# Stage four of a prime-factor Fourier transform in quarter-array matmuls, in a fused mixing and mixture-of-experts kernel

## The chip, the cores and the metric

The kernel runs on one core of one Trainium2 chip. The metric is the device time of one execution in microseconds (us). The kernel before takes 1470.89 us, the median of three runs (1468.29, 1470.89 and 1471.23).

The core has a matmul engine (PE, a 128 by 128 array whose results go to PSUM), three engines for elementwise work (DVE, ACT and POOL), and a queue engine (SP) that starts nearly all transfers (DMAs). PSUM has eight banks of 128 partitions by 512 float32. Everything here is float32. In the profile one matmul of the program shows as two PE instructions, each with a weight load of its own ("PEld").

## The reference

Two blocks follow each other: a filter in the frequency domain along the sequence, then a mixture of experts with one expert for each row.

```python
# x: (8, 2496, 256); filt_r, filt_i: (1249, 256)
X = np.fft.rfft(x, axis=1)
y = np.fft.irfft(X * (filt_r + 1j * filt_i)[None], n=2496, axis=1)

# rows: y as (19968, 256); 8 experts; w1: (8, 256, 1024), w2: (8, 1024, 256)
logits = rows @ w_gate
expert = argmax(logits, axis=1)
gate = softmax(logits)[expert]
out = gate * (relu(rows @ w1[expert]) @ w2[expert])
```

## The kernel before

**The transform.** 2496 is 39 times 64, and 39 and 64 have no common factor, so the transform of one batch is four stages of small matrix products. Stage a multiplies over the 39 (table `tas`), stage b over the 64 (`tbs`) and then with the filter on DVE, stage c goes back over the 64 (`tcs`), and stage d goes back over the 39 (`tds`). The 64 positions along the other axis are taken three at a time: 22 groups, 21 of three positions and one of a single position. A group of three has 3 x 39 = 117 rows of data (`TP`) and 3 x 40 = 120 rows of spectrum (`TK`: 20 cosine and 20 sine parts for each position). One chunk is four groups; a batch has five chunks of four groups and one of two, the last of which holds the single position.

Stage d (`stage_d`, lines 579 to 596) takes a chunk of the spectrum `ui`, 120 partitions by 4 x 256, and issues one matmul for each two groups: 120 rows deep, 128 columns of `tds`, 512 wide, into one PSUM bank. `evac` (line 409) copies the bank to `yo` on DVE or ACT, whichever is planned to be done first. The chunk of two groups issues two matmuls of 256, one 120 deep and one 40 deep, because its second group has only one position.

Between the stages the data goes through DRAM: `zd` after stage a, `ud` after stage c, both written by `move` and read back by `load_z` and `load_u` (lines 514 to 527), all on the queue of SP. Batch 0 stays on the chip instead (`first_a`, `turn_z`, `first_c`, `turn_u`).

**Routing.** For batches 3 to 7 (`by_blocks`), DVE transposes `yo` in 32 by 32 blocks (`turn_y`), `block_logits` multiplies with the gate weights in matmuls that use 32 columns each and lie beside each other on the array (tile `bank<-yt,wb`), and `block_back` turns the logits back. `route` (a generator, line 738 on) finds each row's expert and its place. Then POOL writes each group's rows to `rows` in DRAM, ordered by expert, with one indirect DMA per group (`scatter`), 22 per batch of up to 117 rows. A row of `rows` is 256 values, eight copies of its token's number and eight of its gate (`DR = D + 16`).

**The experts.** `rows_in` loads a tile of up to 512 rows of one expert (the numbers and gates go to `ng`, eight buffers), `weights` loads its weights. Most tiles' first product is seven block products in place of eight (`hidden_by_quarters`), each with an add on DVE out of PSUM (`hT<-bank,hT`), after sums of weights and rows on POOL. The second product is `result`, four row blocks of eight matmuls. Once all transform steps are issued (`late`), tiles of 512 rows take seven block products for it too (`result_by_quarters`), with sums of `w2` on POOL (`w2_sums`, tile `tsum`). Finished rows go to the output by an indirect DMA on POOL (`send`).

**Order of work.** Each engine runs its instructions in order, and the kernel's Python writes that order out. `slot(k)` lists the steps of slot k: stages b and c of batch k, stage a of batch k+1, stage d and routing of batch k-1. A planner (`Order`, lines 125 to 234) keeps an estimated time for each engine; the main loop picks the next step whose data and PSUM bank it expects to be ready, and fills PE between transform steps with expert products, as far as `share` allows. `bank()` hands out the PSUM bank that it expects to be free first. The DMA queue of SP is in order too: an entry that waits for a buffer holds back those behind it.

**The start.** `load_filters(c)` loads four of the 20 filter columns at a time. The real parts go to the first 64 partitions of `ht` and ACT copies them to the other 64 (`turn_z`, line 630). The imaginary parts come in pieces on 64 partitions each; POOL multiplies them with the signs `sgs`, two chunks ahead.

Of the kernel before, what the change touches and what calls it, by code (L numbers as in the profile page):

```python
# [34 lines left out]
TK = NB * NS  # L35
DH = D // P
# [4 lines left out]
NJ = D // CT  # L41

# [13 lines left out]
def dft_tables():  # L56
# [24 lines left out]

    ids = np.zeros((NB, N1, NG))
    valid = np.zeros((NB, N1, NG))
    for j in range(NB):
# [3 lines left out]

    by_block = np.zeros((4, CT, NG + 2))
    by_block.reshape(P, NG + 2)[:TP, :NG] = valid.reshape(TP, NG)  # L90
# [5 lines left out]
        "ta": ta.reshape(TP, TK),  # L96
        "tb": tb,
        "tc": tc,
        "td": np.pad(td.reshape(TK, TP), ((0, 0), (0, P - TP))),
        "sg": np.concatenate([sg[:, :NF // 2], sg[:, NF // 2:]]),  # L100
        "ids": ids.reshape(TP, NG),
        "valid": np.concatenate([np.pad(valid.reshape(TP, NG), ((0, P - TP), (0, 0))), by_block], axis=1),
    }


def lay_x(x):

    out = np.zeros((x.shape[0], P, NG, D), x.dtype)
    q = np.arange(N1)
    for j in range(NB):  # L110
        for i in range(len(range(j, N2, NB))):
            out[:, j * N1:(j + 1) * N1, i] = x[:, token(q, NB * i + j)]
    return out
# [11 lines left out]
class Order:  # L125
# [25 lines left out]
    @staticmethod  # L151
    def parts(a):

        if a.name[:3] != "ht_":
            return [a.name]
        row, at = divmod(a.offset, a.ap[0][0])
        return [f"{a.name}/{h}/{k}" for h in ((0, 1) if a.ap[0][1] == P else (row // (P // 2),))
                for k in range(at // (2 * D), at // (2 * D) + (a.ap[1][1] + 1) // 2)]
# [20 lines left out]
    def count(self, engine, op, args, named):  # L179
# [31 lines left out]
        else:  # L211
            if out is None:
                took = 0.8 if engine == "sync" else 0.02
            elif engine == "tensor":
# [3 lines left out]
                took = max(0.1, 0.00085 * n) if op == "transpose" else max(0.216, 0.00169 * n) if rows > 32 else 0.00045 * n  # L218
                took *= 2.0 if start < self.slow else 1.0
# [31 lines left out]
class Slots:  # L251
# [3 lines left out]
    def freed(self, name, tag):  # L255
# [3 lines left out]
        if tag in self.live and name in self.live[tag]():  # L259
            return 1e9  # L260
# [33 lines left out]
def kernel(  # L294
# [12 lines left out]
    ids: bass.AP,  # L307
    valid: bass.AP,
# [25 lines left out]
    TR = E * TE  # L334

    dram = open_pool(ctx, name="dram", bufs=1, space=DRAM)
    zd = [dram.tile([N2, NS, D], F32, tag=f"z{b % 2}", name="zd") for b in range(B)]
    ud = [dram.tile([N2, NS, D], F32, tag=f"u{b % 2}", name="ud") for b in range(B)]


    DR = D + 16
    rowsd = dram.tile([TR, DR], F32, tag="rows", name="rows")

# [15 lines left out]

    tas = cst.tile([TP, TK], F32, name="tas")  # L360
    tbs = cst.tile([P, P], F32, name="tbs")
    tcs = cst.tile([P, P], F32, name="tcs")
    tds = cst.tile([TK, P], F32, name="tds")
# [15 lines left out]
    ids0 = cst.tile([TP, NG], F32, name="ids0")  # L379
    vld = cst.tile([P, 2 * NG + 2], F32, name="vld")  # L380
# [12 lines left out]
    ps.live["bank"] = lambda: ()  # L393
# [25 lines left out]
    def load_filters(c):  # L419
        f0, n = FH[c]  # L420
        if c == 0:
            nc.sync.dma_start(out=tbs, in_=tb)
            nc.sync.dma_start(out=sgs, in_=sg)
        nc.sync.dma_start(out=ht[:HP, f0:f0 + n], in_=filt[:HP, f0:f0 + n, :])
        half, f1 = divmod(f0, NF // 2)
        rows = slice(half * HP, (half + 1) * HP)
        nh = min(n, NF // 2 - f1)
        parts = [(rows, slice(f1, f1 + nh), slice(NF + f1, NF + f1 + nh))]
        if nh < n:
            parts.append((slice(HP, P), slice(0, n - nh), slice(NF, NF + n - nh)))  # L430
        for r, fs, at in parts:
            nc.sync.dma_start(out=ht[r, at], in_=filt[r, at, :])
            signs.append((c, ht[r, at], sgs[r, fs, None].to_broadcast((HP, fs.stop - fs.start, D))))
        if c == 0:
            nc.sync.dma_start(out=tcs, in_=tcm)

    def load_rest():
        nc.sync.dma_start(out=tds, in_=td)
# [33 lines left out]
    def columns(ap, i0, n):  # L472

        rows = ap.rearrange("t s d -> (t s) d")
        m = min(n, NG - 1 - i0)
        yield TK, slice(0, m), rows[i0 * TK:(i0 + m) * TK, :].rearrange("(i p) d -> p i d", p=TK)
        if m < n:
            yield NS, slice(m, n), rows[(NG - 1) * TK:, :].rearrange("(i p) d -> p i d", p=NS)

# [22 lines left out]
    def by_part(ap):  # L502

        return ap.rearrange("t (c f) d -> (t c) f d", c=2)

# [8 lines left out]
    def load_z(b, c):  # L514
        f0, n = FH[c]
        zi = fin(("z", b, c))
        nc.sync.dma_start(out=zi[:, :n], in_=by_part(zd[b])[:, f0:f0 + n, :])

    def load_u(b, c):
        i0, n = CH[c]  # L520
        ui = fin(("u", b, c))
        for r, m, v in columns(ud[b], i0, n):
# [5 lines left out]

    def stage_a(b, c):
        i0, n = CH[c]  # L530
        xt = ins.pop(("x", b, c))
        zo = sb.tile([TK, 4, D], F32, tag="st", name="zo", bufs=4)
        for j in range(0, n, 2):
            p = bank()
            mm(p[:TK, :], lhsT=tas, rhs=xt[:TP, j:j + 2, :], start=True, stop=True)
            evac(zo[:, j:j + 2, :], p[:TK, :].rearrange("p (t d) -> p t d", t=2), 512)
        for r, m, v in columns(zd[b], i0, n):
# [4 lines left out]
    def stage_b(b, f):  # L542
# [6 lines left out]
        mm(p, lhsT=tbs, rhs=zi[:, j:j + 2, :], start=True, stop=True)  # L549
# [13 lines left out]

    def stage_c(b, f):
# [6 lines left out]
        mm(p, lhsT=tcs, rhs=ys, start=True, stop=True)  # L571
        evac(uo[:, j:j + 2, :], p.rearrange("p (i d) -> p i d", i=2), 512)
        if j == 2:
            f0 = f - 2
            move(by_part(ud[b])[:, f0:f0 + 4, :], uo)
# [3 lines left out]
    def stage_d(b, c):  # L579
# [7 lines left out]
        yo = outs["o", b, c] = sb.tile([P, 4, DR], F32, tag="y", name="yo", bufs=YB)  # L587
        for j in range(0, n, 2):
            p = bank()
            if i0 + j + 2 < NG:  # L590
                mm(p, lhsT=tds, rhs=ui[:TK, j:j + 2, :], start=True, stop=True)
# [6 lines left out]


# [12 lines left out]
    def first_a(c):  # L612
        i0, n = CH[c]
        xt = ins.pop(("x", 0, c))
        for j in range(0, n, 2):
            p = bank()[:, :4 * TK]
            for h in range(DH):
                for i in range(2):
                    mm(p[:, (2 * h + i) * TK:(2 * h + i + 1) * TK], lhsT=xt[:TP, j + i, h * P:(h + 1) * P], rhs=tas,
# [954 lines left out]
```

## Time and profile before

| what | value |
|---|---|
| median of three runs | 1470.89 us |
| the profiled execution | 1474.5 us |
| its span, first to last instruction | 1472.8 us |
| mean granted PE clock | 0.992 |
| PE instructions | 7828, and as many weight loads |
| stage d: matmul instructions 512 wide from `ud` (batches 1 to 7) | 140 |
| stage d: 256 wide, 120 deep and 40 deep | 14 and 14 |
| DVE and ACT copies of `yo` out of PSUM | 6 and 82 |
| scatters to `rows` | 176, and 8 of padding |

The profile is of one execution. Its page gives busy times of each engine, the share of 40 equal slices, the DMA queues, the chain of work that ended last, and groups of instructions with their mean durations. Matmuls overlap: a mean of 606 ns for a matmul instruction contains its way through the array, and the next one starts earlier. What one costs in a row of many is therefore read from the timeline, from one start to the next. Batch 3's first block transposes are at 301.7 us of the span, and stage d of batch 7 reads its last spectrum at 877.1 us, so stage d of batches 3 to 7 lies in the stretch from 300 to 900 us.

### The profile page before, as it was taken

Reading aid. Unit: us, or ns where it says so; the run is one execution under the profiler, and the core shown is the slowest. Engines: PE = TensorE matmul, PEld = TensorE weight load, DVE = VectorE, ACT = ScalarE, POOL = GpSimd, SP = SyncE. Lnnn points to the kernel's source line nnn. Section 1 sums busy time; section 2 is a strip of 40 time slices with the busy share of each in tenths; the row PEclk is TensorE's granted clock in tenths of the full one; section 3 lists DMA queues with packets and bytes.
Section 4 is the critical chain, followed back from the end, with each engine's and each line's share of the span. In section 5 each row is a group of like instructions: output and inputs, shape, how many; then the busy total and the mean of one; then the engine's idle time right before and its main releaser. Section 6 shows DMA issues by size and latency. Waiting matters only on the chain.

```text
span 1472.8 us, 25703 instructions
## 1 busy us (share of the span) xinstructions
PE 1438.4 (98%) x7828; PEld 1148.5 (78%) x7828; DVE 835.8 (57%) x1818; ACT 480.5 (33%) x1005; POOL 818.9 (56%) x1214
## 2 busy tenths in 40 slices
PE   8998999999999999999999999999999999999998
PEld 5553555777577777777787778889999999999997
DVE  4666568335766574566757554566878775531110
ACT  3553443233232333222223232222232322223332
POOL 3434355525456654565375567647989878831111
PEclk9999999999999999999999999999999999999999
DMA  9749798887786576557345644548665424456661
GB/s 255 243 156 339 250 323 257 271 260 222 246 246 189 169 253 180 150 167 251 105 126 151 205 117 132 149 128 244 175 186 154 133 77 139 135 191 176 173 192 42
DMA packets 216383, 278.19 MB, mean 189 GB/s; under 512 B 124131, under 2 KB 163708, under 8 KB 216245
## 3 DMA queue, kind: packets, MB, share of 16 engines
q1 hardware_dynamic: 197125, 233.19, 53.7%
q0 software_dynamic: 19120, 43.33, 8.5%
q8 instruction: 66, 1.08, 0.3%
q14 instruction: 72, 0.59, 0.1%
HBM read 196.45 MB, written 80.64 MB: 188 GB/s over the span
## 4 chain that ended last, share of the span: by engine, by line
PE 85%; DMA 6%; DVE 4%; issue 2%; POOL 1%; SPq 1%; ACT 1%; POOLq 0%; DVEq 0%; ACTq 0%
PE bank L246 85%; DMA fin<-in_x_dram 2%; DMA fin<-ud 2%; DVE yw L246 1%; DVE ys L246 1%; DMA ud<-uo 1%; DMA fin<-zd 1%; SPq L246 1%; POOL out_dram L246 0%; DVE hT L246 0%; DMA w1t<-in_moe_w_dram 0%; DMA ng<-rows 0%; ACT hT L246 0%; DMA zd<-zo 0%; DMA xg<-rows 0%
## 5 line engine op out<-in xcount | busy, mean ns | idle before, releaser
L246 DVE TENSOR_TENSOR hT<-bank,hT 128x512 f32<-128x512 f32 (+1 forms) x504 | 300.8, 626 | 165.4 <-PE bank L246 77.7
L246 PE MATMUL bank<-w2t,hT 128*128 128x256 f32 (+1 forms) x1984 | 387.5, 350 | 2.4 <-DVE hT L246 1.4
L246 PEld LDWEIGHTS bank<-w2t,hT 128*128 128x128 f32 x1984 | 335.1, 190 | 53.0 <-issue 11.7
L246 PE MATMUL bank<-xT,w1t 128*128 128x256 f32 (+1 forms) x1728 | 316.3, 329 | 0.2 <-DVE hT L246 0.2
L246 POOL DMA_INDIRECT out_dram<-ys,ng x161 | 161.5, 1003 | 271.6 <-ACT ys L246 136.7
L246 PEld LDWEIGHTS bank<-xT,w1t 128*128 128x128 f32 x1728 | 265.4, 192 | 32.4 <-issue 8.3
L246 ACT ACTIVATE hT<-hT 128x1024 f32<-128x1024 f32 (+1 forms) x144 | 135.0, 959 | 390.5 <-DVE hT L246 387.5
L246 POOL DMA_INDIRECT rows<-yo,row x176 | 181.9, 1034 | 74.8 <-POOL yo L246 38.5
L246 ACT ACTIVATE ys<-bank,ng 128x256 f32<-128x256 f32 x104 | 49.3, 474 | 303.9 <-PE bank L246 235.2
L246 PE MATMUL bank<-sums,wsum 128*128 128x256 f32 (+1 forms) x576 | 135.6, 358 | 0.0
L246 PE MATMUL bank<-w2s,hT 128*128 x592 | 132.6, 379 | 0.0
L246 PEld LDWEIGHTS bank<-w2s,hT 128*128 128x128 f32 x592 | 110.3, 190 | 13.8
L246 PEld LDWEIGHTS bank<-sums,wsum 128*128 128x128 f32 x576 | 100.5, 190 | 17.7 <-issue 6.8
L246 POOL TENSOR_TENSOR wsum<-w1t 128x256 f32<-128x256 f32 x72 | 56.5, 785 | 82.2 <-PE bank L246 57.7
L246 DVE STREAM_TRANSPOSE xT<-xg 128x512 f32<-128x512 f32 (+2 forms) x126 | 57.4, 493 | 54.6 <-PE bank L246 51.4
L246 DVE TENSOR_TENSOR ys<-bank,ht 128x512 f32<-128x512 f32 x80 | 54.8, 685 | 52.2 <-PE bank L246 42.9
L246 PE MATMUL bank<-fin,tas 117*120 117x512 f32 x154 | 77.3, 622 | 6.9 <-DMA fin<-in_x_dram 6.7
L246 PE MATMUL bank<-fin,tds 120*128 120x512 f32 (+1 forms) x168 | 76.1, 573 | 3.9 <-DMA fin<-ud 3.3
L246 PE MATMUL bank<-fin,tbs 128*128 128x512 f32 x140 | 72.6, 605 | 5.4 <-DMA fin<-zd 5.4
L246 PE MATMUL bank<-ys,tcs 128*128 128x512 f32 x140 | 73.3, 611 | 4.2 <-DVE yw L246 3.4
L246 ACT ACTIVATE hT<-bank 128x128 f32<-128x128 f32 (+1 forms) x191 | 57.6, 303 | 52.5 <-PE bank L246 42.9
L246 PE MATMUL bank<-xT,wsum 128*128 128x256 f32 (+1 forms) x288 | 67.8, 358 | 0.2 <-ACT yo L246 0.2
(171 smaller groups left out, 1766.6 us busy)
## 6 DMA issues: line engine op xcount, KB each, us to landing
w1t<-in_moe_w_dram SPq DMA_DIRECT2D x126, 512.0 KB
w2t<-in_moe_w_dram SPq DMA_DIRECT2D x68, 512.0 KB
fin<-in_x_dram SPq DMA_DIRECT2D x39, 512.0 KB
fin<-zd SPq DMA_DIRECT2D x35, 512.0 KB
ud<-uo SPq DMA_DIRECT2D x35, 512.0 KB
fin<-ud SPq DMA_DIRECT2D x35, 512.0 KB
zd<-zo SPq DMA_DIRECT2D x35, 480.0 KB
xg<-rows SPq DMA_DIRECT2D x112, 128.0 KB
```

What stands on the lines that cost most here:

```text
L246: return real(*args, **named)
```

## The change

- **Stage d of batches 3 to 7** uses the symmetry of cosine and sine. Real and imaginary parts are kept apart: 60 rows each, in partitions 0 to 59 and 64 to 123. Four matmuls of 60 rows by 64 columns, each on another quarter of the array, give the even part and the odd part of the result, for two halves of a chunk (partition halves 0 to 63 and 64 to 127) at once. The output holds 20 of the 39 rows of each position; `fold_y` then forms even plus odd and even minus odd on DVE. `evac` now copies only the odd part, and the even part stays in its PSUM bank until `fold_y` has read it.
- **The layout of u.** `ud` becomes blocks of 64 rows (60 used), `tcs` and `tds` are reloaded with reordered tables at the end of the last slot that uses the old ones, and each store of u becomes two DMAs (126 and 2 partitions). `fill_between` writes the four unused rows of each block once, in slot 1.
- **Scatters.** For batches 3 to 7 each of the 22 scatters has 128 rows. Rows that are no token go to rows behind the table, one each. `DR` is `D + 8`: four copies of number and gate.
- **Filters** are loaded on all 128 partitions, without ACT's copy, and their signs are multiplied on 128 partitions.
- **Stage a** gets the same form under `b >= BA`, but `BA` is 8 and there are batches 0 to 7 only, so it isn't used; its tables for `ta` and `tb` are still loaded late.
- **Smaller:** `ng` has seven buffers; the planner knows the new forms; `open_steps` and `second_products` have slightly different rules.

```diff
+TH = NB * NF
+BA, BD = 8, 3
...
+NW = P * NG - S
+TR = E * (8 * S + P)
...
+                if op == "matmul" and rows == 64 and n > D // 2:
+                    took = 0.29 if n > D else 0.17
...
-    ud = [dram.tile([N2, NS, D], F32, tag=f"u{b % 2}", name="ud") for b in range(B)]
+    ud = [dram.tile([NG * P, D], F32, tag=f"u{b % 2}", name="ud") for b in range(BD)]
+    halves_apart = [dram.tile([NG * P, D], F32, tag=f"v{b}", name="ud") for b in range(2)]
+    ud[BD:] = [halves_apart[b % 2] for b in range(B - BD)]
-    DR = D + 16
+    DR = D + 8
...
-    ps.live["bank"] = lambda: ()
+    ps.live["bank"] = lambda: {p.name for key, p in outs.items() if key[0] == "odd"}
...
-        nc.sync.dma_start(out=ht[:HP, f0:f0 + n], in_=filt[:HP, f0:f0 + n, :])
...
+        nc.sync.dma_start(out=ht[:, f0:f0 + n], in_=filt[:, f0:f0 + n, :])
+        nh = max(0, min(n, NF // 2 - f0))
+        if nh:
+            fs, at = slice(f0, f0 + nh), slice(NF + f0, NF + f0 + nh)
+            nc.sync.dma_start(out=ht[:, at], in_=filt[:, at, :])
+            signs.append((c, ht[:, at], sgs[:, fs, None].to_broadcast((P, nh, D))))
...
+    def by_part(rows, tile, quarters, f0, n):
+        if not quarters:
+            yield tile[:, :n], rows[:N2 * NS].rearrange("(t c f) d -> (t c) f d", c=2, f=NF)[:, f0:f0 + n, :]
+            return
+        m = 2 * (NG - 1)
+        for lo, hi, r in ((0, m * NB, NB), (m * NB, P, 1)):
+            at = rows[lo // NB * 64 + f0, :]
+            to = tile[lo:hi, :n]
+            dims = [[64 * D, (hi - lo) // r]] + ([[NF * D, r]] if r > 1 else []) + [[1, n * D]]
+            yield bass.AP(to.tensor, to.offset, [list(to.ap[0]), [1, n * D]]), bass.AP(at.tensor, at.offset, dims)
...
+    def fill_between():
+        for u in halves_apart:
+            at = u[TH, :]
+            nc.sync.dma_start(out=bass.AP(at.tensor, at.offset, [[64 * D, 2 * NG - 2], [1, 4 * D]]), in_=ht[:2 * NG - 2, :4, :].rearrange("p f d -> p (f d)"))
+            nc.sync.dma_start(out=u[(NG - 1) * P:, :], in_=ht[:, 0, :])
...
+        tds = tables["td"]
+        if b >= BD:
+            m = n // 2
+            both = [bank() for _ in range(2)]
+            for h in range(2):
+                for part in range(2):
+                    k = slice(64 * part, 64 * part + TH)
+                    mm(both[part][64 * h:64 * h + 64, :m * D].rearrange("p (i d) -> p i d", i=m), lhsT=tds[k, :64],
+                       rhs=ui[k, h * m:(h + 1) * m, :], start=True, stop=True)
+            evac(yo[:, m:n, :D], both[1][:, :m * D].rearrange("p (i d) -> p i d", i=m), m * D)
+            outs["odd", b, c] = both[0]
+            return
...
+    def fold_y(b, c):
+        m = CH[c][1] // 2
+        even = outs.pop(("odd", b, c))[:, :m * D].rearrange("p (i d) -> p i d", i=m)
+        yo = outs["o", b, c]
+        nc.vector.tensor_tensor(yo[:, :m, :D], even, yo[:, m:2 * m, :D], op=ALU.add)
+        nc.vector.tensor_tensor(yo[:, m:2 * m, :D], even, yo[:, m:2 * m, :D], op=ALU.subtract)
...
-            nc.scalar.copy(out=ht[HP:, f:f + 4], in_=ht[:HP, f:f + 4])
...
-            nc.vector.tensor_copy(row.rearrange("p (c g) -> p g c", g=4), pr[:, :, 0])
+            nc.vector.scalar_tensor_tensor(
+                out=row.rearrange("p (c g) -> p g c", g=4),
+                in0=lids[:, NG + t0:NG + t0 + wide].rearrange("p (c g) -> p g c", g=4), scalar=float(b * NW),
+                in1=pr[:, :, 0], op0=ALU.add, op1=ALU.max)
...
-            m = N1 if t0 + i == NG - 1 else TP
+            m = P if b >= BD else N1 if t0 + i == NG - 1 else TP
...
-        ng = gis[i] = pools["moe"].tile([P, 4, DR - D], F32, tag="ng", name="ng", bufs=8)
+        ng = gis[i] = pools["moe"].tile([P, 4, DR - D], F32, tag="ng", name="ng", bufs=7)
...
-            if late and i < LARGE:
+            if late and i < LARGE and (wide or i in made):
...
+                if c < nch and k > BD:
+                    steps.append((at + 0.001, lambda c=c: fold_y(k - 1, c), None, 0.0, "y", lambda c=c: [outs["odd", k - 1, c], outs["o", k - 1, c]]))
```

## The prediction

> **What bounds the kernel now.** I read the page first: the busy times, then the chain that ended last.
>
> ```profile
> PE 1438.4 (98%) x7828; PEld 1148.5 (78%) x7828; DVE 835.8 (57%) x1818; ACT 480.5 (33%) x1005; POOL 818.9 (56%) x1214
> PE 85%; DMA 6%; DVE 4%; issue 2%; POOL 1%; SPq 1%; ACT 1%; POOLq 0%; DVEq 0%; ACTq 0%
> ```
>
> PE is the bound. But a busy PE includes the way through the array, so I asked for busy times by stretches of 100 us.
>
> ```profile
> 100.00:200.00 100.00, 90.99 (x327) 48.54 (x327) 64.06 (x159) 42.12 (x94) 44.44 (x74) 0.95 0.90 303
> 700.00:800.00 100.00, 99.21 (x508) 78.18 (x507) 64.54 (x127) 27.51 (x54) 53.76 (x85) 1.00 0.44 123
> 1100.00:1200.00 100.00, 100.00 (x681) 94.01 (x681) 75.93 (x111) 28.99 (x44) 85.77 (x93) 1.00 0.43 129
> ```
>
> The columns after the length are busy PE, PEld, DVE, ACT and POOL, then clock, DMA share and GB/s. Up to 300 us PE waits (9 us in each of the first two stretches), mostly for DMAs: the waits list 8.6 us for x, 5.4 for z, 3.3 for u. From 300 us to the last expert tiles it has no gap: 298.6 of 300, then 297.9 of 300, then 99.7 to 100 of each 100. Expert products fill every hole between the transform's steps. Stage d of batches 3 to 7 lies from 300 to 900 us, so a microsecond of PE work saved there is one off the end, unless new waits eat it. What a matmul costs I read from PE's timeline, from one start to the next.
>
> ```profile
> 602.69 1.88 PE L246 MATMUL bank<-fin,tds 120*128 120x512 f32 x4
> 604.40 1.03 PE L246 MATMUL bank<-sums,wsum 128*128 128x256 f32 x4
> ```
> ```profile
> 779.88 1.22 PE L246 MATMUL bank<-fin,tds 120*128 120x256 f32 x4
> 781.03 1.13 PE L246 MATMUL bank<-fin,tbs 128*128 128x512 f32 x2
> 782.00 3.62 PE L246 MATMUL bank<-w2t,hT 128*128 128x256 f32 x16
> ```
> ```profile
> 831.03 1.03 PE L246 MATMUL bank<-xT,wsum 128*128 128x256 f32 x4
> 831.99 0.64 PE L246 MATMUL bank<-yt,wb 128*32 128x128 f32 x16
> 832.57 1.99 PE L246 MATMUL bank<-xT,w1t 128*128 128x256 f32 x8
> 834.40 1.03 PE L246 MATMUL bank<-sums,wsum 128*128 128x256 f32 x4
> ```
>
> First pair: a full chunk of stage d takes 604.40 - 602.69 = 1.71 us, 0.429 for each of four instructions (256 columns take 0.2165). Second: the last chunk, whose second half is only 40 rows deep, takes 2.12 us to 782.00 with the two `tbs` after it, which alone need 0.86: 1.25 us for 0.87 of streaming. Changing the array's shape there and back costs 0.39. Third: block logits use 32 columns each. From 831.03 to 834.40 are 3.37 us; the 12 full instructions around them need 2.60, so the 16 small ones cost 0.775. One after another they would need 16 x 0.107 = 1.71, four side by side 0.43. So column tiles do run together, and the excursion costs **0.345 us** beyond its streaming (drain in, first weights, drain out, next weights).
>
> **The change part by part.** *Quarters in stage d.* A full chunk has four matmuls, eight instructions of 512 columns on four quarters: if they run together, two waves of 0.429, plus the excursion's 0.345: 1.20 against 1.71. 5 batches x 5 chunks x 0.51 = **-12.8 us**. The last chunk: two waves of 0.2165 + 0.345 = 0.78 against 1.25, 5 x 0.47 = **-2.4 us**. Together -15.2. No row of this trace shows two *row* halves running together; the nearest, block logits, shows only columns. The Trainium skill ("TensorEngine Tiling (Array Packing)", section Tiling Modes) says that 64 by 64 gives four independent tiles which multiply in parallel, provided (Restrictions and Gotchas) that row tiles write different PSUM banks, as they do here; by the rule alone, without its price for the drain, the gain would be 25 x 0.86 + 5 x 0.82 = 25 us. It also says that a change of mode drains the array, which the trace has at 0.345 to 0.39 with the weights. I take the rule for the parallelism and the row for the price. Bounds: -15.2 (with 0.39: -13.9), and +8.5 if the rows take turns (below).
>
> *Evacuation.* The same page (Performance Considerations) speaks against the change: tiling speeds up the matmul and not the emptying of PSUM, which may become the bound. Its price by this trace's rows:
>
> ```profile
> L246 DVE TENSOR_TENSOR hT<-bank,hT 128x512 f32<-128x512 f32 x392 | 257.4, 684 | 124.0 <-PE bank L246 68.7 <-ACT hT L246 42.0 <-issue 0.7
> ...
> L246 ACT COPY yo<-bank 128x512 f32<-128x512 f32 x82 | 47.7, 588 | 36.3 <-PE bank L246 27.7 <-DMA rows<-yo,row 4.4 <-DMA out_dram<-ys,ng 2.6
> ```
>
> Per batch 11 copies of 588 ns become 6, and DVE gets two adds per chunk at the price of `hT`'s: 10 x 0.684 + 2 x 0.42 = 7.7 us. So DVE +38 us and ACT -15 us over five batches. From 300 to 900 us DVE is busy 369 of 600 us (61%); it becomes 68%. From 1100 to 1200 it is at 76% with PE at 100.00, so on average this is hidden. In detail it isn't free: behind the two adds (1.37 us) on DVE are the expert adds that free PSUM banks, stage b's multiplications and the block transposes, and the even part's bank is held 1 to 3 us longer out of eight. PE waits for all of those. Bounds: 0, and 0.5 us for each of the 30 chunks, 15 us; I take **+1.5**, nearer to zero, since the trace's waits for DVE after 300 us sum to about 2 us at a like load.
>
> *Queue of SP.* 25 second stores (two partitions each) minus five loads of 40 rows, four late tables, one list, four fills: 29 entries of 0.43 us (the median of u loads), 12 us in 600. The late tables wait for the last matmul that reads the old ones; behind them stand loads of z, u and weights. SP already waits 462 us for PE in 172 places, the longest 20.5, with PE full, so prefetch covers it: 0, up to 1.5 if a load of u is caught. The fills (0.6 MB) fall between 73 and 110 us, where DMA is 0.48 busy: 0, up to 2.3 if they hit the transfers after 110.
>
> *Scatters.* 176 as before. POOL's time doesn't follow the rows: 1034 ns with mostly 117, 979 for the padding's 128. Bytes: 2816 rows of 1056 B against 2496 of 1088 per batch, 1.3 MB more in all at 0.5 to 0.7 DMA share. POOL's fills of `yo` get narrower (307 to about 260 ns, 30 of them). The last op of `route` reads one operand more (165 ns to perhaps 250, 15 times, DVE). `ng`'s rows of 32 bytes: nothing. Seven buffers: in the tail the last `ng` load is at 1438.1 and its tile is sent at 1467.1, 4.1 tiles of 7.03 us, so five or six live: 0. Together 0, bounds -0.5 and +1.
>
> *Filters.* In the first 36.8 us DMA is 0.96 busy at 255 GB/s, so loads count. 40 pieces of 64 KB on half the partitions (2.56 MB) become 30 of 128 KB (3.84 MB). The first 70 us in 40 slices show 401 and 411 GB/s while only x comes on 128 partitions, and mostly 190 to 260 after the half loads join: 2.56/0.235 = 10.9 us against 3.84/0.4 = 9.6. ACT loses five copies of 1.04, POOL 3 of 6 multiplications (about 4.8 us of 9.7), before stage b of batch 0. Bounds: -2 (also a shorter cold spell), +3.8 if the 1.28 MB come at 340 GB/s on top; I take **-0.5**.
>
> *Late rule.* The first `tsum` is made at 983.6 us, before its tile is current, so the added condition mostly holds: 0. If one tile falls back to the plain product, it costs 64 x 0.2165 - 112 x 0.108 = 1.7.
>
> Sum: -12.8 - 2.4 + 1.5 - 0.5 = **-14.2 us**. The profiled execution took 1474.5 (span 1472.8 and 1.7 around it), which gives 1460.3. It is 3.6 above the median, so for the median 1470.9 - 14.2 = **1457**.
>
> **The rivals.**
>
> *A, the forecast: 1457.* For it: PE is full, and small tiles do run side by side in this trace. Its own range is 1450 to 1466.
>
> *B, slower: the row halves take turns.* Both halves feed the same 64 output columns, and no row here shows them at once. Then a full chunk has four waves: 4 x 0.429 + 0.345 = 2.06, +0.345 each, 25 times +8.6; the last chunk 4 x 0.2165 + 0.345 = 1.21, nearly as before. With the other +1.0: about **1480**. It decides from the point where the streaming of eight instructions takes over 1.37 us (0.86 in A, 1.72 here). Against it stands the skill's statement of independence.
>
> *C, no change: the wait moves to DVE.* If the adds and the held bank cost PE 0.45 us per chunk, 30 chunks give back 13.5: **1470**. For it: three fixed DVE operations in a row (two adds, a transpose of 1.23 us). Against it: PE full at 76% DVE, and 38 us of DVE have 230 us of idle time.
>
> *D, more:* excursions that meet a block of logits share a part of the drains, and the start gains 2 us: **1449**.
>
> *E: the start goes wrong.* Up to 300 us PE waits and its clock drops in four spells (20 us at half clock). Filters that come later, or one more spell, cost 4 to 20 us: **1461 to 1477**.
>
> **How the numbers follow.** A 0.62, C 0.14, B 0.13, D 0.06, E 0.05. 0.2% (2.9 us) is about what a measurement of this kernel can tell from no change. A and D are faster; C splits 0.04 faster, 0.08 same, 0.02 slower; E 0.02 same, 0.03 slower; B slower. Faster 0.72, same 0.10, slower 0.18. The range 1449 to 1475 leaves out B, half of D and a part of E.
>
> **What would show it.** After: 240 matmul instructions of 60 rows by 64 columns (200 of them 512 wide), in two waves of four, an excursion of 1.15 to 1.30 us for a full chunk; four waves mean B. PE's busy time falls by about 15 us, DVE's rises by 30 to 38. In 300 to 900 us PE stays above 99%; if it drops to 97% with waits for DVE, C. PE's first `ys,tcs` chunks and the idle time up to 300 us stay within 3 us; if not, E. I am wrong if the saved time shows in the quarters and the end does not move with it.

## The result, and the profile after

The changed kernel takes 1462.2 us (median of 22 runs, 1456.2 to 1475.5), the kernel before beside it 1469.96 (22 runs, 1467.3 to 1475.1). The ratio is 0.995 with a 95% interval of 0.9936 to 0.9963: 7.4 us less, between 5.4 and 9.4. The sign was as forecast, the size about half of the 14.2.

The profiled execution of the changed kernel took 1461.53 us (span 1459.8), close to its median. That of before took 1474.5, some 4.5 above the median of its 22 runs. So the two spans differ by 13.0 us where the medians differ by 7.8: the pair of profiles flatters the change by about 5 us, and where a phase is read from it, this has to be kept in mind.

First the row of busy times on the page of the changed kernel.

```profile
PE 1420.6 (97%) x7948; PEld 1130.1 (77%) x7948; DVE 871.3 (60%) x1878; ACT 458.2 (31%) x975; POOL 806.7 (55%) x1212
```

PE is down by 17.8 us (a part of it is before's lower clock at the start), DVE up by 35.5, ACT down by 22.3 (15 for the copies of `yo`, the rest mostly its copies of the filters). There are 120 more matmul instructions, as four small ones stand for two. Then PE's timeline around a full chunk and a last chunk of batch 7.

```profile
818.32 0.41 PE L295 MATMUL bank<-sel,ls 128*128 128x32 f32 x2 [0.29 <-ACT ls L295]
818.65 1.09 PE L295 MATMUL bank<-fin,td 60*64 60x512 f32 x8
819.67 1.13 PE L295 MATMUL bank<-xT,wsum 128*128 128x256 f32 x4
820.64 1.89 PE L295 MATMUL bank<-xT,w1t 128*128 128x256 f32 x8
...
845.99 0.66 PE L295 MATMUL bank<-fin,td 60*64 60x256 f32 x8
846.58 1.99 PE L295 MATMUL bank<-xT,w1t 128*128 128x256 f32 x8
```

The eight small instructions occupy 819.67 - 818.65 = 1.02 us. The ordinary product behind them takes 820.64 - 819.67 = 0.97 instead of 4 x 0.2165 = 0.87, so 0.10 more for its first weights. Where an ordinary product stands ahead, the first small instruction starts 309 ns after its last instruction instead of 216: 0.09 of draining. That makes **1.21 us** for a full chunk; 1.20 was forecast, and 1.71 was the price before. The last chunk takes 0.59 + 0.20 = 0.79 (forecast 0.78). The drain is read in front of another chunk: four ordinary products start at 604.96 us, and the quarters behind them at 605.91, after 0.95 us instead of 0.87.

```profile
604.96 1.03 PE L295 MATMUL bank<-w2t,hT 128*128 128x256 f32 x4
605.91 0.66 PE L295 MATMUL bank<-fin,td 60*64 60x512 f32 x4
```

Inside the group at 818.65 the trace has starts at 0, 7, 14 and 20 ns and then four at 480 to 500 ns: two waves of four, here from two narrow windows on PE.

```profile
818.65 0.66 PE L295 MATMUL bank<-fin,td 60*64 60x512 f32 x4
```
```profile
819.13 0.61 PE L295 MATMUL bank<-fin,td 60*64 60x512 f32 x4
```

The groups of DVE and PE give the counts.

```profile
L295 DVE TENSOR_TENSOR yo<-bank,yo 128x512 f32<-128x512 f32 x50 | 34.2, 686 | 2.1 <-ACT yo L295 1.0
L295 DVE TENSOR_TENSOR yo<-bank,yo 128x256 f32<-128x256 f32 x10 | 4.2, 421 | 0.5 <-ACT yo L295 0.3
```
```profile
L295 PE MATMUL bank<-fin,td 60*64 60x512 f32 x200 | 27.0, 613 | 3.0 <-DMA fin<-zd 3.0
...
L295 PE MATMUL bank<-fin,td 60*64 60x256 f32 x40 | 3.3, 402 | 0.0
```

The fold costs DVE 34.2 + 4.2 = 38.4 us. So the parts have the forecast size: 25 x 0.50 + 5 x (1.25 - 0.79) = 14.8 us taken off PE. What is missing must be found in waits. The stretch from 300 to 900 us holds nearly all of stage d of batches 3 to 7, though not all as was written above: before, the first two chunks of batch 3 start at 287.0 and 297.4 us, and after, the first three of the 30 chunks in quarters at 256.0, 280.0 and 295.3. In the kernel before and after it reads (length, then busy PE, PEld, DVE, ACT, POOL, then clock, DMA share, GB/s):

```profile
300.00:900.00 600.00, 596.45 (x2986) 453.05 (x2985) 368.92 (x791) 185.14 (x371) 335.53 (x525) 1.00 0.62 187
```
```profile
300.00:900.00 600.00, 592.88 (x3131) 448.31 (x3130) 406.43 (x865) 170.24 (x343) 343.70 (x549) 1.00 0.63 190
```

DVE's share rises from 61% to 68% as forecast, and PE's idle time from 3.6 to 7.1 us. PE is at 98.8%, between the 99% and the 97% that were to tell the forecast from rival C. And late in the kernel stands a wait that was 0.3 us before:

```profile
998.95 1.03 PE L295 MATMUL bank<-xT,wsum 128*128 128x256 f32 x4
1002.91 2.05 PE L295 MATMUL bank<-w2t,hT 128*128 128x128 f32 x16 [2.94 <-POOL w2t L295]
```

PE waits here for POOL's sums of `w2`.

To see gaps that are too short for the idle column, I added up, over all of PE's matmul instructions, the time to the next start less the streaming (0.427 us for 512 columns, a quarter of that for each of four small tiles that run together; streaming at half clock counts as a gap too). From 300 to 1200 us these gaps sum to 44.2 us before and 58.9 after; up to 300 us to 47.3 and 44.2; from 1200 us on to 7.6 and 7.3. Of the 30 chunks in quarters 27 start after 300 us, and two of them stand in a row (at 800.9 us) and cost one excursion together, so the excursions explain 26 x 0.353 = 9.2 of the 58.9; before it is 5 x 0.39 = 2.0 of the 44.2. What is left over I call stalls: 42.2 before, 49.7 after. This ledger is used for every experiment below.

### The profile page after: what moved, and what is told of

The parts are those of the page before. It is cut to its first block, busy times and chain, and to the rows that moved or that the text cites. A ratio compares the mean times of both kernels' runs of the same rounds, so it can differ in the third digit from the quotient of the medians.

```text
span 1459.8 us, 25997 instructions
## 1 busy us (share of the span) xinstructions
PE 1420.6 (97%) x7948; PEld 1130.1 (77%) x7948; DVE 871.3 (60%) x1878; ACT 458.2 (31%) x975; POOL 806.7 (55%) x1212
## 3 DMA queue, kind: packets, MB, share of 16 engines
q1 hardware_dynamic: 198930, 235.20, 54.5%
## 5 line engine op out<-in xcount | busy, mean ns | idle before, releaser
L295 PEld LDWEIGHTS bank<-w2t,hT 128*128 128x128 f32 x1984 | 336.6, 191 | 57.1 <-issue 12.6
L295 ACT ACTIVATE ys<-bank,ng 128x256 f32<-128x256 f32 x96 | 45.4, 473 | 283.7 <-PE bank L295 234.3
L295 PE MATMUL bank<-fin,ta 117*120 117x512 f32 x154 | 75.2, 607 | 1.5 <-DMA fin<-in_x_dram 1.5
L295 PE MATMUL bank<-fin,tb 128*128 128x512 f32 x140 | 73.6, 614 | 3.0 <-DMA fin<-zd 1.6
L295 PE MATMUL bank<-ys,tc 128*128 128x512 f32 x140 | 72.9, 606 | 3.5 <-DVE ys L295 3.5
L295 ACT ACTIVATE hT<-bank 128x128 f32<-128x128 f32 (+1 forms) x193 | 58.1, 303 | 57.6 <-PE bank L295 47.3
L295 PE MATMUL bank<-sums,w1t 128*128 128x256 f32 (+1 forms) x288 | 67.3, 356 | 0.0
```

Of the source, the lines that this page charges most:

```text
L295: return real(*args, **named)
```

## The experiments

The expectations name theories as they came up. Theory 1: the new filters make the start 5 to 6 us shorter, and the quarters keep only about half of their saving on PE. Theory 2: the filters are worth the forecast 0.5 us, and the early lead of the one profile after is a spell of half clock that fell otherwise. Theory P: the quarters have their full worth, but the written order that goes with each kernel takes a part back. Theory F: the old filters are simply better behind the new layout. Theory D: the work that the fold puts on DVE eats most of what the quarters save (rival C). All ratios are against the kernel before on the same chip, four experiments to a chip in the order told here, n is the number of runs, and a ratio's distance from 1 is turned into us with the 1469.1 to 1469.5 us that the kernel before took beside them. The changed kernel was timed in the first measurement only, not beside the experiments.

| kernel | gaps to 300 us | 300 to 1200 us | excursions after 300 us | stalls left |
|---|---|---|---|---|
| before | 47.3 | 44.2 | 2.0 | 42.2 |
| filters alone | 39.2 | 44.1 | 2.0 | 42.1 |
| after | 44.2 | 58.9 | 9.2 | 49.7 |
| after with old filters | 47.4 | 52.9 | 9.2 | 43.7 |
| whole array | 41.4 | 37.7 | 0 | 37.7 |
| whole array, old filters | 49.8 | 37.5 | 0 | 37.5 |
| first add three times | 45.5 | 79.2 | 9.5 | 69.7 |
| other `HOP`, quarters | 50.3 | 56.4 | 8.8 | 47.6 |
| other `HOP`, whole array | 54.5 | 39.6 | 0 | 39.6 |
| half of the fold on POOL | 45.1 | 51.3 | 9.2 | 42.1 |
| the same, old filters | 49.5 | 51.3 | 9.5 | 41.8 |
| whole array with the fold's load | 41.3 | 48.7 | 0 | 48.7 |
| stage a in quarters too | 47.4 | 58.6 | 12.4 | 46.2 |

Four pairs in this table differ in the filter loads only, and within each pair PE's instructions stand in exactly the same order; on the other engines only the filters and a few operations between 17 and 43 us differ. In three of the pairs the gaps from 300 to 1200 us agree within 0.2 us. The time by which one profile is ahead of the other, instruction by instruction, hardly moves: 8.71 us at 302 us and 8.44 near the end (filters alone against before), 9.01 and 8.80 (whole array), 4.81 and 4.70 (fold on POOL); in between it stays within 0.6 us. So in these three pairs the written order fixes the time after 300 us, and what differs between executions is made before. The fourth pair, after against the old filters in it, is the exception, and that is where the missing time of this profile was found.

**Filters alone, on the kernel before.**

```diff
-        nc.sync.dma_start(out=ht[:HP, f0:f0 + n], in_=filt[:HP, f0:f0 + n, :])
...
+        nc.sync.dma_start(out=ht[:, f0:f0 + n], in_=filt[:, f0:f0 + n, :])
...
-            nc.scalar.copy(out=ht[HP:, f:f + 4], in_=ht[:HP, f:f + 4])
```

> The kernel before with nothing but the filters' loads of the change (all 128 partitions, no copy on ACT, signs on 128 partitions). Theory 1 (the start is 5 to 6 us shorter because the half-partition loads held up the x chunk behind them, and the quarters keep only half of their PE saving): 1464 to 1465 us against 1470, and PE's last matmul with zi as its operand near 45.5 us of the span, not 51.4. Theory 2 (the filters are worth the 0.5 us of the prediction, and the early lead in the one profile after is a clock spell that fell otherwise): 1469 to 1470 us.

Measured: 1466.07 (n 11), ratio 0.9982 (0.9972 to 0.9993): 2.6 us less, between the two theories and more than the forecast 0.5. The rates of the forecast came out: from 12 to 28 us the DMAs move 413 GB/s where they moved 234 with the half loads (before, then with the new filters), and PE has no gap there.

```profile
12.00:28.00 16.00, 13.07 (x62) 8.56 (x62) 3.93 (x9) 6.62 (x12) 3.77 (x2) 0.81 1.05 234
```
```profile
12.00:28.00 16.00, 16.00 (x90) 11.10 (x90) 8.94 (x16) 8.00 (x18) 6.42 (x5) 1.00 1.03 413
```

PE's last product with `zi` starts at 45.2 us, as theory 1 had it, against 51.4. The profile is 8.7 us ahead of before's at 302 us; but before's profile is 5.4 us above the median of the runs beside this one, so about 3 of that is left for the medians.

**The old filters in the changed kernel.** The same edit backwards, on the kernel after.

> The changed kernel with the filters' loads of before. Theory 1: 1466 to 1468 us, that is 5 us over the changed kernel's 1462, zi's last matmul near 51.4 us. Theory 2: 1462 to 1463 us.

Measured: 1455.72 (n 5), ratio 0.9907 (0.9891 to 0.9923). That is 13.7 us less than before, and some 6 us less than the change with its new filters. It missed every expectation. As the order of work is the same, the two traces can be laid over each other, matmul by matmul. Just ahead of 292.3 us the changed kernel is 4.6 us *ahead* of this one. It gives that back at small products of routing (`bank<-sel,ls`), in six steps of 0.2 to 1.3 us, 4.3 in all, and is level at 990 us. At the wait for `w2t` shown above it falls 3.0 behind: POOL got a load of `w1t` 1.6 us later, two of its operations behind that took 1.8 us more (1.71 for 0.74 and 1.79 for 0.99), and the sums stand behind both. The loss at `sel,ls` looks like this. First PE and ACT in the changed kernel:

```profile
848.51 0.64 PE L295 MATMUL bank<-yt,wb 128*32 128x128 f32 x16
849.08 1.13 PE L295 MATMUL bank<-sums,wsum 128*128 128x256 f32 x4
850.05 1.03 PE L295 MATMUL bank<-xT,w1t 128*128 128x256 f32 x4
852.06 0.41 PE L295 MATMUL bank<-sel,ls 128*128 128x32 f32 x2 [0.98 <-ACT ls L295]
```
```profile
851.74 0.27 ACT L295 COPY ls<-bank 128x128 f32<-128x128 f32 x1 [3.40 <-PE bank L295]
```

And the same place with the old filters:

```profile
850.45 0.64 PE L296 MATMUL bank<-yt,wb 128*32 128x128 f32 x16
...
852.86 0.30 PE L296 MATMUL bank<-sel,ls 128*128 128x32 f32 x2
```
```profile
851.22 0.27 ACT L296 COPY ls<-bank 128x128 f32<-128x128 f32 x1 [0.94 <-PE bank L296]
```

With the old filters ACT copies the logits 0.13 us after the block product ends (851.22 against 850.45 + 0.64). In the changed kernel ACT is idle too, the block product ends at 849.15, and the copy starts 2.6 us later, so PE stops. From the last small matmul's start to the copy it is 0.3 to 0.4 us where all is well; in the changed kernel's profile 9 of the 30 copies take 1.3 to 2.9 us with their engine idle. In the profile of before, from the same first measurement, there are 3 (1.0 to 1.9 us, which cost PE nothing); in the twelve profiles of the experiments there is none. The first of the six steps, 1.3 us, lies ahead of 300 us; the other five, 3.0 us together, and the 3.0 at `w2t` are the 6.0 us by which the gaps from 300 to 1200 us differ. No theory had foreseen the late copies.

**Stage d as one whole-array matmul again, all else as after.**

```diff
-            both = [bank() for _ in range(2)]
-            for h in range(2):
...
-            outs["odd", b, c] = both[0]
+            for j in range(0, n, 2):
+                p = bank()
+                mm(p, lhsT=tds, rhs=ui[:, j:j + 2, :], start=True, stop=True)
+                evac(yo[:, j:j + 2, :D], p.rearrange("p (i d) -> p i d", i=2), 512)
```

The table holds the sum and the difference at once, so there is nothing to fold.

> The changed kernel with stage d of batches 3 to 7 as one matmul over the whole array for each two groups (124 rows by 128 columns, the sum and the difference in the table), copied by evac; no quarters, no fold. All else of the change stays: layout of u, two stores, 128-row scatters, tables, filters. By the rows of the profile after it has 25 x 0.50 + 5 x 0.08 = 12.9 us more on PE, and 38 us less on DVE. If nothing else were lost (the prediction): 1462 + 14 - 1.5 = 1474 to 1475 us. Theory 1 (quarters keep about half): 1467 to 1470 us. A rival in which the losses come from the new layout, the scatters or SP's queue and not from the fold: 1475 us, since those stay.

Measured: 1463.35 (n 7), ratio 0.9966 (0.9953 to 0.9979), lower than all expectations. By working the quarters take 25 x (1.71 - 1.21) + 5 x (0.86 - 0.79) = 12.9 us off PE against this kernel. Against the kernel with quarters and the old filters (0.9907) it is 8.7 us behind, against the changed kernel (0.995) only 2.4. This order has 37.7 us of stalls, 6.0 fewer than quarters with the old filters: that is the price of fold, held bank and the order that goes with them, by the ledger. And it is 4.5 fewer than before, while on PE it saves only 5 x (1.25 - 0.86) = 2 us against it: most of its 5 us come from fewer stalls in its own order.

**A stricter rule for the late block form.**

```diff
-            if late and i < LARGE and (wide or i in made):
+            if late and i < LARGE and (wide or i in made and not making):
```

> The changed kernel, but the first tile after the transform takes the block form of its second product only if all four sums of w2 on POOL are already issued. In the profile after PE waits 2.9 and 0.35 us at 997 to 1003 us for those sums; the plain product costs 1.7 us more of PE. If the wait is what is lost: 1460.5 us, with no wait for tsum or w2t. If the wait only moves: 1462 to 1464 us.

Measured: 1474.95 (n 11), ratio 1.0039 (1.0028 to 1.005). No tile took the block form of the second product any more (7516 PE instructions, 9 x 48 fewer). In this kernel the plain products of the tiles whose `w2` sums POOL had begun read weights that were already partly turned into sums, so its results are wrong. Nine tiles at the 1.7 us of the prediction are 15.3 us; the time rose by 13. That fits the size of the block form, but PE waited 5.8 us for `w2t` all the same, so it says nothing on the wait at 1002.9.

This run tells something else. Up to 985 us every engine has the same instructions in the same order as in the changed kernel, the new filters among them, and none of its copies of `ls` is late. Here are the block product and the copy that were 2.6 us apart in the changed kernel, first PE and then ACT:

```profile
851.87 0.65 PE L295 MATMUL bank<-yt,wb 128*32 128x128 f32 x16
```
```profile
852.63 0.27 ACT L295 COPY ls<-bank 128x128 f32<-128x128 f32 x1 [0.94 <-PE bank L295]
```

The copy starts 0.11 us after the product. Still this profile loses 2.5 us against the old filters between 302 and 988 us: 1.0 at a spell of half clock at 410 us, which the changed kernel's profile has too, and 1.5 from 825 us on, where PE waits 2.80 us for DVE (1.94 with the old filters) and then runs four products in the time of eight:

```profile
825.87 1.12 PE L295 MATMUL bank<-sums,wsum 128*128 128x256 f32 x4 [2.80 <-DVE hT L295]
826.81 1.89 PE L295 MATMUL bank<-xT,w1t 128*128 128x256 f32 x4
```

**Whole array with the old filters.** Both edits together.

> Stage d of batches 3 to 7 over the whole array, as in the run before, with the filters' loads of before. With the new filters the quarters were worth 1.1 us (1463.35 against 1462.2), with the old ones the changed kernel came to 1455.7. If the quarters have a worth of their own that the new filters spoil only by the order of work that comes with them (theory P): 1464 to 1468 us here, so that the quarters are worth 8 to 12 us with the old filters. If the old filters are simply better behind the new layout (theory F): 1457 us, and the quarters are worth 1 us here too.

Measured: 1463.78 (n 12), ratio 0.996 (0.9941 to 0.9979), close to theory P; theory F is out. The new filters make no difference to this kernel that could be told from noise. Quarters are worth 0.996 - 0.9907, or 7.8 us, with the old filters. By the ledger it is 23.5 us of streaming, less 15.4 by which the gaps after 300 us grow (52.9 against 37.5: 9.2 of excursions and 6.2 of stalls), less 1.1 for the three excursions before: 7.0.

**The first add of the fold three times.** Its result is the same each time; DVE gets 38 us more.

```diff
+        for _ in range(3):
+            nc.vector.tensor_tensor(yo[:, :m, :D], even, yo[:, m:2 * m, :D], op=ALU.add)
```

> The changed kernel with the first of the two adds of the fold done three times over (same result): 60 more DVE operations, 38 us more on DVE, as much again as the fold costs. If DVE's load is what ate the gain (theory D): the same loss again, 1468 us or more. If not: within 3 us of 1462.

Measured: 1478.35 (n 11), ratio 1.0059 (1.004 to 1.0077): 16 us more than the changed kernel. So DVE's idle microseconds do not hide 38 more, as theory D had it. The mean clock over the runs is 0.9865, against 0.993 for the changed kernel; (1 - clock) x span is 19.9 us against 10.3, so up to 9.6 of the 16 is PE at half clock, and the rest are the stops themselves. From 300 to 1200 us its profile has five spells at half clock, the changed kernel's has one; the one at 734.6 us begins between the two stops below. How it reaches PE is seen in the timelines of PE and DVE of this kernel.

```profile
728.63 1.02 PE L295 MATMUL bank<-ys,tc 128*128 128x512 f32 x2
732.48 0.26 PE L295 MATMUL bank<-rx,sel 128*32 128x16 f32 x8 [2.83 <-DVE yo L295]
735.70 1.08 PE L295 MATMUL bank<-yt,wb 128*32 128x128 f32 x16 [2.96 <-DVE yw L295]
```
```profile
729.57 2.86 DVE L295 TENSOR_TENSOR yo<-bank,yo 128x512 f32<-128x512 f32 x4
732.34 1.23 DVE L295 STREAM_TRANSPOSE yt<-yo 128x1024 f32<-128x1024 f32 x1
733.50 0.65 DVE L295 TENSOR_TENSOR ys<-bank,ht 128x512 f32<-128x512 f32 x1
734.17 0.69 DVE L295 SCALAR_TENSOR_TENSOR yw<-bank,ht 64x512 f32<-64x512 f32 x1
734.87 0.68 DVE L295 TENSOR_TENSOR yw<-bank,ht 64x512 f32<-64x512 f32 x1
735.59 0.69 DVE L295 TENSOR_TENSOR ys<-ys,yw 128x512 f32<-128x512 f32 x1
```

Four fold operations in a row take 2.86 us, and PE stands until they are done (732.4). Then the transpose and the filter's operations follow, and PE stands 2.96 us more, until the third of those, which reads a bank, is done. DVE has no gap there, though its average is 72% (432.76 of 600).

**Another written order.** The planner adds a constant, `HOP`, to the time at which it expects an operand to be ready on another engine. Only the order of instructions depends on it.

```diff
-    HOP = 0.1
+    HOP = 0.15
```

With the quarters:

> The changed kernel with one constant of the planner changed: it reckons 0.15 us, not 0.10, from one engine's result to the next engine. No instruction is added or taken away; only the order differs. Theory P: another time, anywhere from 1454 to 1465 us; waits for ACT's copy of the logits (5.4 us in the profile after) should get fewer. Theory D or F: 1461 to 1463 us.

And with the whole array:

> The kernel with whole-array stage d and the new filters with the same planner constant 0.15. Theory P: 1459 to 1468 us, by its own accident. Whether the quarters are worth something under this order is the difference to the run with quarters and 0.15: the forecast says 13, theory D about 1.

Measured: 1468.06 (n 12), ratio 0.9998 (0.9983 to 1.0013), and 1474.07 (n 12), ratio 1.0025 (1.0009 to 1.0042), both above every expectation. The whole-array kernel loses 8.7 us by the constant alone, and the quarters with it are 13 us above the kernel with quarters that lost nothing to late copies. The ledger places it: after 300 us the stalls are only 1.9 (whole array) and 3.9 us up, and the gaps up to 300 us, where only 4 of the 30 chunks run, are the highest of all (54.5 and 50.3). As these two profiles are 2.4 above and 3.1 below their medians, a usual start has about 52 and 53 us of gaps, against 44 and 45 with the old constant. Between the two the quarters are worth 4.0 us by the ratios and 6.0 by the medians; the ledger gives 23.5 - 16.8 - 1.4 = 5.3 (streaming, gaps after 300 us, the four excursions before). So the order of the start alone, some 8 us, moves this kernel by as much as the change did.

**Half of the fold on POOL.** The odd table is doubled; DVE forms even plus half the odd part out of PSUM, and POOL subtracts the odd part from the result.

```diff
-        nc.vector.tensor_tensor(yo[:, :m, :D], even, yo[:, m:2 * m, :D], op=ALU.add)
-        nc.vector.tensor_tensor(yo[:, m:2 * m, :D], even, yo[:, m:2 * m, :D], op=ALU.subtract)
+        nc.vector.scalar_tensor_tensor(out=yo[:, :m, :D], in0=yo[:, m:2 * m, :D], scalar=0.5, in1=even, op0=ALU.mult, op1=ALU.add)
+        nc.gpsimd.tensor_tensor(yo[:, m:2 * m, :D], yo[:, :m, :D], yo[:, m:2 * m, :D], op=ALU.subtract)
```

> The changed kernel with the second half of the fold on POOL: the odd table is doubled, DVE forms even plus half of that in one operation, and POOL takes the doubled odd part off for the other half. Same result; 30 DVE operations (19 us) fewer, 38 us more on POOL, and the even part's bank is free one operation earlier. Theory D (the fold's DVE operations cost PE waits): 1456 to 1459 us. If the loss is an accident of the order alone: 1462, give or take 4. If POOL becomes the bound: over 1465 us.

Measured: 1455.8 (n 5), ratio 0.9911 (0.9897 to 0.9925): 5.7 us less than the changed kernel, about where theory D had it. But against quarters with the old filters, which had no late copies, it is equal: 1.6 us of stalls are saved, and one tile less has the block form of the second product (8 in place of 9, 1.7 us).

**The whole array with the fold's load.** No quarters; where the fold stood, DVE takes the maximum of `yo` with itself, twice per chunk.

```diff
+        for part in (slice(0, m), slice(m, 2 * m)):
+            nc.vector.tensor_tensor(yo[:, part, :D], yo[:, part, :D], yo[:, part, :D], op=ALU.max)
```

> Stage d over the whole array (1463.35 us) plus two DVE operations for each chunk of the size of the fold's, in its places in the order, which change nothing: DVE has the fold's load, PE has no quarters. Theory D: the load alone costs 7 to 12 us, so 1470 to 1475 us. If it costs nothing without the quarters: 1463 to 1465 us, and it is the quarters' held bank that matters.

Measured: 1474.38 (n 5), ratio 1.0034 (1.0021 to 1.0047): 10 us more than the same kernel without these operations, of which 1.7 are one tile less in the block form. The ledger has 11.0 more of stalls. DVE's load alone can thus cost that much in this order, as theory D said. The longest stop of PE in that stretch, in the timelines of PE, ACT and DVE:

```profile
692.91 1.03 PE L292 MATMUL bank<-sums,wsum 128*128 128x256 f32 x4
698.54 2.07 PE L292 MATMUL bank<-sums,w1t 128*128 128x256 f32 x4 [4.60 <-ACT yo L292]
```
```profile
697.82 0.17 ACT L292 COPY gts<-bank 128x8 f32<-128x8 f32 x1 [6.34 <-DVE row L292]
697.90 1.07 ACT L292 COPY yo<-bank 128x512 f32<-128x512 f32 x2
```
```profile
688.92 0.68 DVE L292 TENSOR_TENSOR ys<-bank,ht 128x512 f32<-128x512 f32 x1
...
691.65 1.30 DVE L292 STREAM_TRANSPOSE xT<-xg 128x512 f32<-128x512 f32 x2
...
696.18 1.48 DVE L292 TENSOR_TENSOR hT<-bank,hT 128x512 f32<-128x512 f32 x2
697.57 0.16 DVE L292 SCALAR_TENSOR_TENSOR row<-lids,bank 128x8 uint32<-128x8 f32 x1
```

Read it backwards. PE names ACT, but ACT was idle for 6.34 us: its small copy of the gates waited for `row`, the last operation of routing on DVE, and ACT's copies of `yo` stood behind that small copy and kept their banks. `row` is a matter of 0.16 us, but DVE had 8.6 us of filter operations, transposes and expert adds ahead of it without a gap. The releaser that the wait names is three links away from its cause.

**Half of the fold on POOL, with the old filters.**

> The fold half on POOL, with the filters' loads of before (1455.7 us with the fold on DVE). Theory D: 1451 to 1454 us, better than both kernels. If POOL takes back what DVE gives: 1455 to 1458 us.

Measured: 1457.62 (n 6), ratio 0.9916 (0.9889 to 0.9944), no gain over 0.9907 with the fold on DVE, and the gaps from 300 to 1200 us are those of its twin with the new filters to 0.1 us. Theory D fails here: the half of the fold that moved was not what the changed kernel lost by.

**Stage a in quarters too, for batches 6 and 7.**

```diff
-BA, BD = 8, 3
+BA, BD = 6, 3
```

> The changed kernel with its own switch set so that stage a of batches 6 and 7 is in quarters too. By PE alone: 2 x (5 x 0.51 + 0.08) = 5.3 us less, 1457 us. Theory D: its folds of x put about 15 us more on DVE, which costs as much or more: 1461 to 1468 us.

Measured: 1450.7 (n 4), ratio 0.9864 (0.9845 to 0.9882), 20 us under the kernel before, 12.6 under the changed one, and 6.3 under the same quarters of stage d with the old filters: the best version of this study. Again both expectations missed, and theory D's by far: DVE is as loaded as with the triple adds.

```profile
300.00:900.00 600.00, 594.11 (x3235) 450.17 (x3234) 430.71 (x916) 172.80 (x358) 355.32 (x560) 1.00 0.65 195
```

430.71 us of DVE against 432.76, yet the stalls are 46.2 us here and 69.7 there. Against the old filters in the changed kernel, the quarters of stage a take 9.4 us of streaming off PE, one tile more has the block form (1.7), and the gaps after 300 us grow by 5.7: together 5.4 of the 6.3.

## Why the prediction was right in sign and half in size

**The sum.** Chunk by chunk the streaming falls by 25 x 0.854 + 5 x 0.427 = 23.5 us. From 300 to 1200 us the gaps add 14.7: 9.2 - 2.0 = 7.2 of excursions and 7.5 of stalls. The tail adds -0.3. The gaps up to 300 us, three excursions among them, are 3.1 lower in the pair of profiles; as before's profile is 4.5 above its median and after's 0.7 below, for the medians that is +2.1, if these distances come from the start. Together -7.0; measured are -7.4 by the ratio and -7.8 by the medians. So nearly the whole is accounted for. The last sign of being wrong that the forecast named came half true: the saved time shows in the quarters, and the end moved by half of it.

**Row halves run together; -15.2 (right).** Two waves of four, 1.21 us for 1.20 forecast, -14.8 by measured prices. Rival B is excluded; it asked 2.06. Shared drains, part of rival D, occur once in stage d (two chunks in a row at 800.9 us).

**Evacuation, +1.5 (the term that failed in this measurement).** Stalls came out at +7.5. But most of that is not what the term was about: in the kernel with the same order on PE and the old filters they are +1.5 against before, and the whole change then gives -13.7, as the sum without the filters said. The other 6 us are, in this profile, the late copies of `ls` and the wait for `w2t`. Rival C, 0.45 us per chunk on DVE, is thus not the cause of these 6 us. Its mechanism is real: against the same stage d without a fold, quarters stall 4.3 to 8.0 us more (in the changed kernel 12.0), the fold's operations alone cost 10 us in one order, and another 38 us of them cost 16. That the term comes out at its size with the old filters is luck: it does so because before's own order stalled 4.5 us more than the whole-array kernel's. I took an average DVE share of 68% for proof of slack; it is none.

**Why the copies came late (open).** ACT and DVE were idle and the matmuls before them had ended by the records. Neither the order nor the new filters are enough to bring it about: the kernel with the stricter late rule has both up to 985 us, and none of its copies is late. Before's profile from the first measurement has the same in a weak form. That speaks for the chip or the hour of that measurement rather than for the change. But the changed kernel itself was not run beside the others, so this is argued and not shown. Nor is it shown that late copies and the wait for `w2t` are what separates the medians, 1462.2 and 1455.7 from two measurements. Over its 22 runs the changed kernel's mean clock is 0.9930, with the old filters it is 0.9946; by (1 - clock) x span that alone is 2.4 us of the 6.5. And the stricter late rule shows that this order can lose 2.5 us after 300 us without one late copy.

**Filters, -0.5 (bounds held for all but the lone test).** -2.6 alone, +0.9 in the whole-array kernel, and with half of the fold on POOL -0.7: within the scatter of the start. The 6 us of the first comparison are not shown to be theirs: in the two profiles the changed kernel was 4.6 us ahead when its copies began to come late.

**The late rule, 0 (wrong in the profiled execution).** 3.3 us of waits for the sums of `w2`, 0.3 before. The condition held; the sums were late.

**Fills, second stores, scatters, 0.** Not separated. With the typical start 2 us worse than before's, the bound of 2.3 for the fills is not excluded, and neither is a small share of rival E.

## What to carry to other kernels

Lay two traces with the same instruction order over each other before giving a difference a cause: here it showed that a loss of 6 us, which fitted the story of a loaded DVE, lay at a handful of copies that came late and at one wait for POOL. When a change pays for smaller matmuls with elementwise work, price that work where it meets the rest of its engine's queue, and look for who stands behind it; the same fold of 38 us on DVE went with 6.0, 8.0 or 11 us of stalls by the order it met. Where a program writes its own order, a constant in the planner moves the time as much as a real change, so time variants side by side on one chip, and set each profiled execution against its own median first.

## What was not expected of the hardware

Over 1100 us of full PE, the two executions of three pairs with one order keep their distance within 0.6 us; nearly all of the difference between them is made in the first 300 us. Against that stand the copies of `ls` that start 1.3 to 2.9 us after the matmul that releases them, and the spell of half clock at 826.8 us in one run and not in two others of the same order.

Four 60 by 64 float32 tiles start within 20 ns of each other, and the second wave comes 480 ns after the first: 429 of streaming and some 50 by which the first wave is longer (0.64 us for each instruction, 0.59 in the second). The weights of the second wave are not what it waits for: all eight loads of the group are done 0.21 us after its start.

```profile
818.65 0.21 PEld L295 LDWEIGHTS bank<-fin,td 60*64 60x64 f32 x8
```

Where two chunks stand in a row, the third and the fourth wave each come 429 ns after the one ahead. When two groups of small tiles stand back to back they share a drain: in the kernel with stage a in quarters, PE's timeline has both kinds in a row.

```profile
564.02 1.09 PE L295 MATMUL bank<-fin,ta 60*64 60x512 f32 x8
564.93 1.04 PE L295 MATMUL bank<-fin,td 60*64 60x512 f32 x8
```

The first takes 0.91 us where the lone chunk took 1.02, plus the 0.10 that the next ordinary product would have lost.
